# Numerator, denominator and transpose of attention among the Q projections, all operand sums on VectorE, weight sums a stage ahead

## The chip, the cores and the metric

The kernel runs on one core of one Trainium2 chip, with its own TensorE (matmuls, "PE" in the profile; its weight loads are "PEld"), VectorE ("DVE"), ScalarE ("ACT"), GpSimd ("POOL") and SyncE ("SP", which only issues transfers). The metric is the device time of one launch in microseconds. Runs shown are several executions of the same program; one further execution was recorded by the profiler, and all durations come from that one.

## What is computed

The reference is a pre-norm block with linear attention, followed by a token-mixing MLP. S = 2048 tokens, D = 1024, 32 heads of 32, F = 3584, all in bf16:

```python
qkv = (x @ wqkv) -> q, k, v per head
phi = lambda t: where(t > 0, t + 1, exp(t)) + 1e-6
pq, pk = phi(q), phi(k)
kv  = einsum("bhsd,bhse->bhde", pk, v)
z   = sum over s of pk
num = einsum("bhqd,bhde->bhqe", pq, kv)
den = einsum("bhqd,bhd->bhq", pq, z) + 1e-6
A   = (num / den) @ wo

h  = x + A(layernorm(x))
# B: layernorm again, then the MLP mixes over the tokens
u  = gelu(einsum("bsd,sf->bdf", layernorm(layernorm(h)), w1) + b1)
y  = einsum("bdf,fs->bds", u, w2) + b2
out = h + transpose(y)
```

## The kernel before

All matrices are cut into tiles of 128 partitions; S has 16 row tiles (`NS`), D has 8 (`ND`), F has 28 (14 pairs, `NFP`). One matmul instruction takes 128 x 128 weights and streams 512 columns. The stages follow each other on TensorE:

1. **K and V** (L187 to L279). Each row tile of x is loaded, normalised and transposed into `xnT`, four tiles by TensorE and twelve by a transposing DMA (L210). Then 8 matmuls for each of four column chunks give K and V. `phi_evac` (L135) makes phi with two ScalarE and two VectorE instructions. `kv_accum` sums kv and z in PSUM over all tiles.
2. **Q** (`q_unit`, L282). 32 units of 8 matmuls, (u, j) for 4 token chunks u of 512 and 8 column blocks j. Each writes `pqT[:, j, chunk u]`, which is phi(q), transposed. Four units come before the weights of attention (`ndrhs`, L304 to L306) are made. L402 to L420 issue the others: all but the last four, then two attention blocks, then the last four units.
3. **Attention and output projection** (loop at L435). For a row tile i, `attn_num_den` (L321) does 8 small matmuls into the one PSUM tile `nd_ps`, then a ScalarE copy of the denominators, a reciprocal (L339) and three multiplications (L344) on VectorE into `o_sb`. `attn_transpose` turns `o_sb` by DMA into a tile `oT`. `out_proj` (L364) seeds two PSUM tiles with x (L372), does 2 x 8 matmuls with `oT` as weights (L374), copies the result to `h_bf` (L384), takes statistics (L385, L386) and stores h to DRAM from GpSimd's queue (L390). `normalize_h` (L394) writes `hE` for even tiles and `hO` for odd ones, and after each odd tile `combine` (L126) makes the five sums that the next stage streams: on GpSimd for the first seven pairs, on VectorE for the last.
4. **W1** and 5. **W2** (`Strassen`, L464; `run_pair`, L554). Each is a product done by Strassen's scheme: per pair of output tiles seven products m1 to m7 instead of eight. Products 1, 2, 5, 6 and 7 need a sum of two weight tiles (`asum`, L474, VectorE, into the rotating tile `sa` of the pool `sapool`, or `sb2` for W2). A product is 8 matmuls in W1 and 14 in W2, so a pair is 56 or 98 matmuls, and each stage is 784. The results are added between PSUM tiles W, X, Y and Z on VectorE. In W1 the Gelu on ScalarE writes `gE` and `gO`, and `combine` on VectorE makes four of the five streamed sums of W2; the fifth, `gT1`, is made at L622 on GpSimd in 14 pieces, after W1 and before W2. The first pair of each stage is split (`first`): all k but the last of m2, m3 and m1 run ahead of the last k, which is the one that is ready last. The last product of a pair, m7, runs inside the next pair.

The order of the source is not the order of issue. At build time a planner puts the instructions of each engine in order by their readiness in its own model, with earlier lines first among those that are ready, and gives out tiles and waits. Tiles of a pool opened after another was closed reuse its memory and wait for its users: `hE`, `hO` and the W1 weights give way to the W2 weights, `gT1` and the output tiles.

The names that matter below: `pqT` (phi of q, 8 planes of 2048 columns), `o_sb`, `oT`, `hst` (statistics), `hE`/`hO`, `hT1`, `hT3`, `hT4` (combined), `sa` (weight sums), `gT1` (shown as gT_4077), `w1p`/`w2p` (weights), `hr` (h read back for the output), `xr` (x for the residual).

Of the kernel before, what the change touches and what calls it, by code (L numbers as in the profile page):

```python
# [8 lines left out]
P = 128  # L9
# [11 lines left out]
BANK = 512  # L21
# [5 lines left out]
def kernel(  # L27
# [116 lines left out]
    h_dram = [dram.tile([P, D], BF16, name=f"h_dram{i}") for i in range(NS)]  # L144
    mctx = ctx.enter_context(ExitStack())

    with ExitStack() as actx:
        a3s = actx.enter_context(tc.tile_pool(name="a3s", bufs=4))
        a3w = actx.enter_context(tc.tile_pool(name="a3w", bufs=3))
        otsb = actx.enter_context(tc.tile_pool(name="otsb", bufs=3))  # L150
# [156 lines left out]

        w1pool = mctx.enter_context(tc.tile_pool(name="w1pool", bufs=3, side="right"))
# [9 lines left out]
        with ExitStack() as a3:  # L318
# [33 lines left out]
            def attn_transpose(o_sb):  # L352
                oT = otsb.tile([P, ND, P], BF16, name="oT")
                nc.sync.dma_start_transpose(out=oT[:], in_=o_sb[:])
                return oT
# [8 lines left out]
            def out_proj(i, oT):  # L364
# [4 lines left out]
                for dc in range(NDC):  # L369
# [3 lines left out]
                    for j in range(ND):  # L373
                        nc.tensor.matmul(  # L374
                            ap_[:, 0:CW],
                            lhsT=oT[:, j, :],
                            rhs=wo_sb[:, j, dc * CW:(dc + 1) * CW],
                            start=(j == 0 and not SEED_RESIDUAL),
                            stop=(j == ND - 1 and SEED_RESIDUAL),
                            skip_group_check=SEED_RESIDUAL,  # L380
                        )
# [8 lines left out]
                nc.gpsimd.dma_start(h_dram[i][:], h_bf[:])  # L390
# [3 lines left out]
            def normalize_h(i):  # L394
                dst = hE if i % 2 == 0 else hO
                nc.vector.tensor_scalar(dst[:, i // 2, :], h_bfs.pop(i)[:], mv_all[:, i, 0:1], sc_all[:, i:i + 1], ALU.subtract, ALU.mult)  # L396
# [4 lines left out]
            HOLD = 4  # L401
            rest = q_units[4:]  # L402
            n_early = max(0, len(rest) - HOLD)
            for (u, j) in rest[:n_early]:
                q_unit(u, j)
            done_u = 0
            if len(q_units) - HOLD > 0:
                done_u = (len(q_units) - HOLD) // ND
            n_pro = min(NS, (done_u * SW) // P)
            LA3 = 2  # L410
            osb = {}
            oTs = {}
            pro_nd = min(LA3, n_pro)
            pro_tr = min(LA3 - 1, n_pro)
            for i in range(pro_nd):
                osb[i] = attn_num_den(i)
            for i in range(pro_tr):
                oTs[i] = attn_transpose(osb.pop(i))
            for (u, j) in rest[n_early:]:
                q_unit(u, j)  # L420
# [10 lines left out]
            for i in range(pro_nd, min(LA3, NS)):  # L431
                osb[i] = attn_num_den(i)
            for i in range(pro_tr, min(LA3 - 1, NS)):
                oTs[i] = attn_transpose(osb.pop(i))
# [15 lines left out]
    psy = ctx.enter_context(tc.tile_pool(name="psy", bufs=NT, space=PSUM))  # L450
    psw = ctx.enter_context(tc.tile_pool(name="psw", bufs=NT, space=PSUM))
    psz = ctx.enter_context(tc.tile_pool(name="psz", bufs=NT, space=PSUM))
    psx = ctx.enter_context(tc.tile_pool(name="psx", bufs=NT, space=PSUM))
# [5 lines left out]
    cpool = ctx.enter_context(tc.tile_pool(name="cpool", bufs=2))  # L459
    w2a = ctx.enter_context(tc.tile_pool(name="w2a", bufs=1))  # L460
    sactx = ExitStack()
    sapool = sactx.enter_context(tc.tile_pool(name="sapool", bufs=6))

    class Strassen:  # L464
        def __init__(self, wt, nk, sap, mov, evac):
            self.wt, self.nk, self.sap, self.mov, self.evac = wt, nk, sap, mov, evac
            v = wt[:].rearrange("p (k two) (h f) -> p k two h f", two=2, h=2)
            self.a11 = v[:, :, 0, 0, :]
            self.a12 = v[:, :, 1, 0, :]
            self.a21 = v[:, :, 0, 1, :]  # L470
            self.a22 = v[:, :, 1, 1, :]
            self.sa = {3: self.a11, 4: self.a22}

        def asum(self, m):  # L474
            a, b, op = {
                1: (self.a11, self.a22, ALU.add),
                2: (self.a21, self.a22, ALU.add),
                5: (self.a11, self.a12, ALU.add),
                6: (self.a21, self.a11, ALU.subtract),
                7: (self.a12, self.a22, ALU.subtract),  # L480
            }[m]
            t = self.sap.tile([P, self.nk, P], FP16, tag="sa", name="sa")
            nc.vector.tensor_tensor(t[:], a, b, op)  # L483
            self.sa[m] = t

        def mm(self, m, ps, start, stop, ks=None):
            sa, mv = self.sa[m], self.mov[m]
            for k in range(self.nk) if ks is None else ks:
                nc.tensor.matmul(  # L489
                    ps[:],  # L490
                    lhsT=sa[:, k, :],
                    rhs=mv(k),
                    start=(start and k == 0),
                    stop=(stop and k == self.nk - 1),
                    skip_group_check=True,
                )

        def m2(self, ks=None):
            if ks is None or ks[0] == 0:
                self.W = psw.tile([P, BANK], F32, tag="w", name="psW")  # L500
            self.mm(2, self.W, True, True, ks)
            if ks is None or ks[-1] == self.nk - 1:
                self.s2 = cpool.tile([P, BANK], F32, tag="s2", name="s2")
                nc.scalar.copy(self.s2[:], self.W[:])

        def m3(self, ks=None):
            if ks is None or ks[0] == 0:
                self.Z = psz.tile([P, BANK], F32, tag="z", name="psZ")
            self.mm(3, self.Z, True, True, ks)
            if ks is None or ks[-1] == self.nk - 1:  # L510
                self.d = cpool.tile([P, BANK], F32, tag="d", name="dd")
                nc.vector.tensor_tensor(self.d[:], self.Z[:], self.s2[:], ALU.subtract)

        def m1(self, ks=None):
            if ks is None or ks[0] == 0:
                self.X = psx.tile([P, BANK], F32, tag="x", name="psX")
            self.mm(1, self.X, True, True, ks)
            if ks is None or ks[-1] == self.nk - 1:
                self.Y = psy.tile([P, BANK], F32, tag="y", name="psY")
                nc.vector.tensor_tensor(self.Y[:], self.X[:], self.d[:], ALU.add)  # L520

        def m4(self):
            self.mm(4, self.W, False, True)
            self.t = cpool.tile([P, BANK], F32, tag="t", name="tt")
            nc.vector.tensor_tensor(self.t[:], self.W[:], self.d[:], ALU.add)  # L525
            self.evac(1, 0, self.W)

        def m5(self):
            self.mm(5, self.Z, False, True)
            nc.vector.tensor_tensor(self.t[:], self.t[:], self.Z[:], ALU.subtract)  # L530
            nc.vector.tensor_tensor(self.X[:], self.X[:], self.t[:], ALU.add)
            self.evac(0, 1, self.Z)

        def m6(self):
            self.mm(6, self.Y, False, True)
            self.evac(1, 1, self.Y)

        def m7(self):
            self.mm(7, self.X, False, True)
            self.evac(0, 0, self.X)  # L540

    def moving(E, O, T1, T3, T4):
        lo, hi = slice(0, CW), slice(CW, 2 * CW)
        return {
            1: lambda k: T1[:, k, :],
            2: lambda k: E[:, k, lo],
            3: lambda k: T3[:, k, :],
            4: lambda k: T4[:, k, :],
            5: lambda k: O[:, k, hi],
            6: lambda k: E[:, k, hi],  # L550
            7: lambda k: O[:, k, lo],
        }

    def run_pair(st, nxt, first, pending):  # L554
        if first:
            head = list(range(st.nk - 1))
            st.m2(head)
            st.m3(head)
            st.m1(head)
            last = [st.nk - 1]  # L560
            st.m2(last)
# [121 lines left out]
```

## Time and profile before

| What | Value |
|---|---|
| Median of 3 runs | 629.95 us (628.68 to 631.11) |
| The profiled execution | 633.12 us, of which its span (first to last instruction) is 631.3 |
| TensorE busy | 591.0 us, 94%, 2882 matmuls |
| VectorE busy | 362.6 us, 57% |
| ScalarE busy | 193.1 us, 31% |
| GpSimd busy | 71.2 us, 11% |
| Mean granted TensorE clock | 0.981 |

The page's picture of the span in 40 slices of 15.8 us shows where the engines work (tenths of each slice; PEclk is the granted clock in tenths):

```profile
PE   2998999999997988869999999999679999999997
DVE  6594112136448799876666667665935654565433
ACT  2554444446666556423223222222000000000000
POOL 1000000000000577620000000000840000000000
PEclk9999999999999899979999999999969999999999
```

A row of a view of windows reads: the stretch in us from the span's start, its length, then for PE, PEld, DVE, ACT and POOL the busy time with the number of instructions, the granted clock, and the transfers' share and rate. A row of a group reads: line, engine, operation, what is written and read, shapes, count, then busy us, mean ns of one, and the engine's idle time ahead of them with what ended it. A row of the timeline reads: start, duration, engine, line, operation, and in brackets the idle time before it. In the chain, a row is a start, a duration and what ran.

A busy TensorE is not the same as a full one: matmuls are pipelined and recorded longer than their spacing, so only the distance of starts gives the cost of one.

### The profile page before, as it was taken

Reading aid. Unit: us, or ns where it says so; the run is one execution under the profiler, and the core shown is the slowest. Engines: PE = TensorE matmul, PEld = TensorE weight load, DVE = VectorE, ACT = ScalarE, POOL = GpSimd, SP = SyncE. Lnnn points to the kernel's source line nnn. Section 1 sums busy time; section 2 is a strip of 40 time slices with the busy share of each in tenths; the row PEclk is TensorE's granted clock in tenths of the full one; section 3 lists DMA queues with packets and bytes.
Section 4 is the critical chain, followed back from the end, with each engine's and each line's share of the span. In section 5 each row is a group of like instructions: output and inputs, shape, how many; then the busy total and the mean of one; then the engine's idle time right before and its main releaser. Section 6 shows DMA issues by size and latency. Waiting matters only on the chain.

```text
span 631.3 us, 7530 instructions
## 1 busy us (share of the span) xinstructions
PE 591.0 (94%) x2882; PEld 273.0 (43%) x2882; DVE 362.6 (57%) x684; ACT 193.1 (31%) x384; POOL 71.2 (11%) x73
## 2 busy tenths in 40 slices
PE   2998999999997988869999999999679999999997
PEld 2454444444443444424444444444224444444443
DVE  6594112136448799876666667665935654565433
ACT  2554444446666556423223222222000000000000
POOL 1000000000000577620000000000840000000000
PEclk9999999999999899979999999999969999999999
DMA  9989000007009677404233234200926664351200
GB/s 292 340 198 220 1 0 1 2 0 196 6 0 213 173 165 187 114 29 122 67 105 95 66 86 114 67 2 0 239 69 175 159 166 129 98 158 44 57 26 33
DMA packets 108500, 66.56 MB, mean 105 GB/s; under 512 B 31650, under 2 KB 101296, under 8 KB 108464
## 3 DMA queue, kind: packets, MB, share of 16 engines
q1 hardware_dynamic: 107120, 61.88, 38.2%
q0 software_dynamic: 1344, 4.21, 1.8%
q8 instruction: 22, 0.36, 0.3%
q14 instruction: 14, 0.11, 0.1%
HBM read 50.34 MB, written 8.39 MB: 93 GB/s over the span
## 4 chain that ended last, share of the span: by engine, by line
PE 75%; DVE 10%; POOL 3%; DMA 3%; ACT 2%; issue 1%; POOLq 0%; DVEq 0%; SPq 0%
PE psW L489 15%; PE psX L489 15%; PE psZ L489 15%; PE acc_t L215 12%; PE acc_t L285 8%; PE psY L489 8%; POOL gT_4077 L622 3%; DVE hE L396 3%; DVE hst L385 3%; DVE o_sb L344 2%; DMA oT<-o_sb 1%; PE acc_t L374 1%; DMA x_sb<-in_A_x_dram 1%; DVE st L195 1%; DMA xnT<-xn 1%
## 5 line engine op out<-in xcount | busy, mean ns | idle before, releaser
L489 PEld LDWEIGHTS <-sa 128*128 128x128 f16 x1120 | 110.0, 98 | 152.1 <-issue 20.8
L215 PE MATMUL acc_t<-wkv,xnT 128*128 128x512 bf16 x512 | 115.2, 383 | 0.0
L215 PEld LDWEIGHTS <-xnT 128*128 128x128 bf16 x512 | 49.9, 99 | 56.8 <-issue 1.1
L140 DVE TENSOR_SCALAR e_sb<-e_sb 128x512 bf16<-128x512 bf16 x64 | 18.7, 292 | 84.4 <-ACT e_sb L137 84.3
L374 PE MATMUL acc_t<-wo_sb,oT 128*128 128x512 bf16 x256 | 59.4, 387 | 3.4 <-DMA oT<-o_sb 3.4
L483 DVE TENSOR_TENSOR sa<-w1p 128x1024 f16<-128x1024 bf16 x70 | 47.7, 684 | 21.2 <-PE psX L489 12.4
L285 PE MATMUL acc_t<-xnT,wq_sb 128*128 128x512 bf16 x256 | 56.1, 379 | 0.0
L483 DVE TENSOR_TENSOR sa<-w2p 128x1792 f16<-128x1792 bf16 x40 | 47.8, 1202 | 14.4 <-PE psW L489 13.7
L137 ACT ACTIVATE e_sb<-acc_t 128x512 bf16<-128x512 f32 x64 | 38.2, 597 | 52.5 <-PE acc_t L215 31.8
L622 POOL TENSOR_TENSOR gT_4077<-gE,gO 128x512 f16<-128x512 f16 x14 | 21.2, 1548 | 170.9 <-PE psX L489 170.9
L374 PEld LDWEIGHTS <-oT 128*128 128x128 bf16 x256 | 24.8, 99 | 31.9 <-DMA oT<-o_sb 4.1
L139 ACT ACTIVATE r_sb<-acc_t 128x512 bf16<-128x512 f32 x64 | 37.9, 592 | 0.0
L285 PEld LDWEIGHTS <-wq_sb 128*128 128x128 bf16 x256 | 24.9, 98 | 29.3
L489 PE MATMUL psX<-gT_4077,sa 128*128 128x512 f16 x112 | 28.8, 394 | 9.3 <-POOL gT_4077 L622 8.0
L489 PEld LDWEIGHTS <-w2p 128*128 128x128 bf16 x224 | 22.3, 100 | 27.7 <-issue 2.2
L525 DVE TENSOR_TENSOR tt<-psW,dd 128x512 f32<-128x512 f32 x22 | 15.2, 692 | 31.9 <-PE psW L489 31.8
L489 PEld LDWEIGHTS <-w1p 128*128 128x128 bf16 x224 | 21.9, 98 | 26.4
L489 PE MATMUL psW<-hE,sa 128*128 128x512 f16 x112 | 28.3, 395 | 4.4 <-DVE hst L385 4.4
L520 DVE TENSOR_TENSOR psY<-psX,dd 128x512 f32<-128x512 f32 x22 | 15.4, 699 | 25.2 <-PE psX L489 25.2
L489 PE MATMUL psZ<-hT_1947,w1p 128*128 128x512 f16 x112 | 26.8, 379 | 0.9 <-POOL hT_1947 L130 0.9
L489 PE MATMUL psX<-hT_1946,sa 128*128 128x512 f16 x112 | 27.0, 383 | 0.0
L489 PE MATMUL psW<-gT_2812,w2p 128*128 128x512 f16 x112 | 26.6, 391 | 0.0
(205 smaller groups left out, 712.4 us busy)
## 6 DMA issues: line engine op xcount, KB each, us to landing
w1p<-in_B_w_dram SPq DMA_DIRECT2D x14, 1024.0 KB, 5.7
w2p<-in_B_w_dram SPq DMA_DIRECT2D x8, 1792.0 KB, 8.4
x_sb<-in_A_x_dram SPq DMA_DIRECT2D x16, 256.0 KB, 6.3
xr<-in_A_x_dram SPq DMA_DIRECT2D x16, 256.0 KB, 2.9
wkv<-in_A_wqkv_dram SPq DMA_DIRECT2D x3, 1024.0 KB, 12.0
wq_sb<-in_A_wqkv_dram SPq DMA_DIRECT2D x2, 1024.0 KB, 12.0
wo_sb<-in_A_wo_dram SPq DMA_DIRECT2D x2, 1024.0 KB, 8.7
wkv<-in_A_wqkv_dram SPq DMA_DIRECT2D x2, 512.0 KB, 6.3
```

The lines of the kernel that those rows point to most:

```text
L137: nc.scalar.activation(e_sb[:], src, ACT.Exp)
L139: nc.scalar.activation(r_sb[:], src, ACT.Relu)
L140: nc.vector.tensor_scalar(e_sb[:], e_sb[:], 1.0, PHI_EPS, ALU.min, ALU.add)
L215: nc.tensor.matmul(pp[:, 0:CW], lhsT=xnT[:, kt, i * P:(i + 1) * P], rhs=wkv[:, kt, c * CW:(c + 1) * CW], start=(kt == 0), stop=(kt == ND - 1),
L285: nc.tensor.matmul(qp[:, 0:SW], lhsT=wq_sb[:, kt, j * P:(j + 1) * P], rhs=xnT[:, kt, u * SW:(u + 1) * SW], start=(kt == 0), stop=(kt == ND ...
L374: nc.tensor.matmul(ap_[:, 0:CW], lhsT=oT[:, j, :], rhs=wo_sb[:, j, dc * CW:(dc + 1) * CW], start=(j == 0 and not SEED_RESIDUAL), stop=(j = ...
L385: nc.vector.bn_stats(st[:, dc, :], ap_[:, 0:CW])
L396: nc.vector.tensor_scalar(dst[:, i // 2, :], h_bfs.pop(i)[:], mv_all[:, i, 0:1], sc_all[:, i:i + 1], ALU.subtract, ALU.mult)
L483: nc.vector.tensor_tensor(t[:], a, b, op)
L489: nc.tensor.matmul(ps[:], lhsT=sa[:, k, :], rhs=mv(k), start=(start and k == 0), stop=(stop and k == self.nk - 1), skip_group_check=True,)
L520: nc.vector.tensor_tensor(self.Y[:], self.X[:], self.d[:], ALU.add)
L622: nc.gpsimd.tensor_tensor(gT1[:, p, :], gE[:, p, 0:CW], gO[:, p, CW:2 * CW], ALU.add)
```

## The change

The change touches four things.

- **Attention.** The Q units run in one loop. After every second unit of the chunks u = 1, 2 and 3 comes `attn(i)` (numerator, denominator, division and transpose) for one row tile of the chunk before: 12 of the 16. The last four stand in the projection loop at i = 0, 2, 4 and 6. The transposing DMA writes into `pqT`, over the columns it came from; the tile `oT` and its pool are gone, and `out_proj` takes its weights from `pqT`.
- **Sums.** `combine` is on VectorE for all pairs. `gT1` is made on VectorE in two pieces of seven tiles, instead of 14 on GpSimd. h is stored from SP's queue.
- **Weight sums ahead.** One pool `sapool` with 5 slots (before: 6, and 6 more for W2) is opened before the W1 weights and lives through both MLP stages. The sums of the first W1 pair stand in the projection loop at i = 10; those of the first W2 pair stand around the last m7 of W1.
- **Waits on memory.** Some pools wait by tile (`reuse_waits="tile"`), PSUM pools are opened in another order, `cpool` has one copy of each tile instead of two, the first W2 pair is not split, and `hr` is loaded at the start of its pair. The class `Strassen` moves up in the file; but for `asum` and the pool argument it is unchanged.

```diff
+            def attn_transpose(i, o_sb):
+                nc.sync.dma_start_transpose(out=pqT[:, :, i * P:(i + 1) * P], in_=o_sb[:])
...
-                            lhsT=oT[:, j, :],
+                            lhsT=pqT[:, j, i * P:(i + 1) * P],
...
-                nc.gpsimd.dma_start(h_dram[i][:], h_bf[:])
+                nc.sync.dma_start(h_dram[i][:], h_bf[:])
...
-                    combine(nc.vector if q == NSP - 1 else nc.gpsimd, hE[:, q, :], hO[:, q, :], hT1[:, q, :], hT3[:, q, :], hT4[:, q, :])
+                    combine(nc.vector, hE[:, q, :], hO[:, q, :], hT1[:, q, :], hT3[:, q, :], hT4[:, q, :])
+
+            def attn(i):
+                attn_transpose(i, attn_num_den(i))
+
+            TPC = SW // P
+            for (u, j) in q_units[4:]:
                 q_unit(u, j)
+                if u >= 1 and j % 2 == 1:
+                    attn((u - 1) * TPC + j // 2)
             xctx.close()
...
             for i in range(NS):
-                if i + LA3 < NS:
-                    osb[i + LA3] = attn_num_den(i + LA3)
-                if i + LA3 - 1 < NS:
-                    oTs[i + LA3 - 1] = attn_transpose(osb.pop(i + LA3 - 1))
+                if i % 2 == 0 and i // 2 < TPC:
+                    attn(NS - TPC + i // 2)
                 if i + 2 < NS:
                     load_xr(i + 2)
-                out_proj(i, oTs.pop(i))
+                out_proj(i)
                 if i >= 2:
                     normalize_h(i - 2)
+                if i == NS - 6:
+                    cur = mk1(0)
+                    for m in (2, 1, 5, 6, 7):
+                        cur.asum(m)
...
+    psy = ctx.enter_context(tc.tile_pool(name="psy", bufs=NT, space=PSUM, reuse_waits="tile"))
+    psx = ctx.enter_context(tc.tile_pool(name="psx", bufs=NT, space=PSUM, reuse_waits="tile"))
+    psw = ctx.enter_context(tc.tile_pool(name="psw", bufs=NT, space=PSUM, reuse_waits="tile"))
+    psz = ctx.enter_context(tc.tile_pool(name="psz", bufs=NT, space=PSUM, reuse_waits="tile"))
...
-    cpool = ctx.enter_context(tc.tile_pool(name="cpool", bufs=2))
+    cpool = ctx.enter_context(tc.tile_pool(name="cpool", bufs=1))
...
+    nxt = mk2(0)
+    for m in (2, 1, 5, 6):
+        nxt.asum(m)
     pend.m7()
-    sactx.close()
+    nxt.asum(7)
     mctx.close()
...
-    for p in range(NFP):
-        nc.gpsimd.tensor_tensor(gT1[:, p, :], gE[:, p, 0:CW], gO[:, p, CW:2 * CW], ALU.add)
+    half = NFP // 2
+    for sl in (slice(0, half), slice(half, NFP)):
+        nc.vector.tensor_tensor(gT1[:, sl, :], gE[:, sl, 0:CW], gO[:, sl, CW:2 * CW], ALU.add)
...
-        run_pair(cur, nxt, p == 0, pend)
+        cur.evac.prefetch()
+        run_pair(cur, nxt, False, pend)
```

More of the change, by code (lines that the diff above doesn't have):

```diff
@@ L362, in load_xr, with out_proj @@
                 xrs[i] = xr
-            def out_proj(i, oT):
+            def out_proj(i):
                 xr = xrs.pop(i)
@@ L458 @@
     gT4 = gpool.tile([P, NFP, CW], FP16, name="gT4")
-    cpool = ctx.enter_context(tc.tile_pool(name="cpool", bufs=2))
+    cpool = ctx.enter_context(tc.tile_pool(name="cpool", bufs=1))
     w2a = ctx.enter_context(tc.tile_pool(name="w2a", bufs=1))
[L461 to L540, printed above, removed]
@@ L597 @@
-    cur = mk1(0)
-    for m in (2, 1, 5, 6, 7):
-        cur.asum(m)
+    hmov.update(moving(hE, hO, hT1, hT3, hT4))
     pend = None
```

243 lines of the change are left out of this document (140 added, 103 removed).

## The prediction

> **What bounds the kernel now.** I first cut the run at its stage borders (windows: length, then busy time and instructions of PE, PEld, DVE, ACT and POOL, then the granted clock).
>
> ```profile
> span 631.3 us, 7530 instructions
> 136.48:193.97 57.49, 57.38 (x290) 26.79 (x289) 30.07 (x98) 35.96 (x68) 0.00 (x0) 1.00 0.27 64
> 193.97:266.89 72.92, 64.25 (x363) 30.88 (x361) 63.19 (x122) 41.33 (x104) 42.02 (x45) 0.98 0.74 175
> 266.89:274.07 7.18, 1.84 (x9) 0.69 (x8) 6.51 (x6) 1.46 (x4) 6.13 (x7) 0.78 0.16 63
> 274.07:443.70 169.63, 169.63 (x778) 76.56 (x778) 108.69 (x194) 47.67 (x72) 0.00 (x0) 0.99 0.26 69
> 443.70:465.93 22.23, 12.90 (x44) 4.19 (x42) 15.57 (x10) 1.27 (x2) 21.17 (x14) 0.76 0.77 201
> 465.93:627.60 161.67, 161.66 (x743) 72.75 (x740) 82.32 (x105) 4.11 (x7) 0.00 (x0) 0.99 0.38 104
> ```
>
> Q projections, most of W1 and most of W2 have a full TensorE. Time is lost in three places: the output projection (193.97 to 266.89), the start of W1 and the start of W2. These are also the only places where GpSimd works and where the clock falls below 0.98. To price the losses I need the real cost of a matmul, since busy time overlaps. From the chain and the timeline:
>
> ```profile
> 286.59 1.73 PE psX L489 x8
> 440.26 1.73 PE psY L489 x8
> 242.95 3.62 PE L374 MATMUL acc_t<-wo_sb,oT 128*128 128x512 bf16 x16
> 246.41 0.63 PE L323 MATMUL nd_ps<-ndrhs,pqT 128*128 128x132 bf16 x8
> 246.88 3.61 PE L374 MATMUL acc_t<-wo_sb,oT 128*128 128x512 bf16 x16
> 443.56 1.46 PE L489 MATMUL psZ<-gT_2811,w2p 128*128 128x512 f16 x6
> ```
>
> Between the first two rows lie 89 blocks of eight: 153.67/712 = 0.216 us per 512-column matmul. One numerator and denominator set takes 0.47 us (246.41 to 246.88). So:
> - output projection: 256 matmuls (55.3) and 13 of the 16 sets (6.1) make 61.4 of 72.92: **11.5 lost**;
> - W1, from 266.89 to 443.56: 784 matmuls are 169.3 of 176.7: **7.4 lost**;
> - W2, from 443.56 to 627.60: 169.3 of 184.0: **14.7 lost**.
>
> Together 33.6 us. Who holds TensorE there (waits in the two stretches, then VectorE's groups from 193.97 to 274.07):
>
> ```profile
> PEld L323 <- DVE o_sb L344: 8.7, 8, 2.1
> PE acc_t L374 <- DMA oT<-o_sb: 3.4, 1, 3.4
> PE psX L489 <- POOL gT_4077 L622: 8.0, 8, 1.6
> L385 DVE BATCH_NORM_STATS2 hst<-acc_t 128x6 f32<-128x512 f32 x32 | 22.0, 690 | 6.4 <-ACT h_bf L384 6.4
> L396 DVE TENSOR_SCALAR hE<-h_bf,mv_all,sc_all 128x1024 f16<-128x1024 bf16 x8 | 19.2, 2394 | 0.6 <-ACT sc_all L389 0.6
> L396 DVE TENSOR_SCALAR hO<-h_bf,mv_all,sc_all 128x1024 f16<-128x1024 bf16 x7 | 3.7, 529 | 0.0
> L386 DVE BATCH_NORM_AGGREGATE mv_all<-hst 128x2 f32<-128x12 f32 x16 | 2.7, 166 | 0.1
> ```
>
> VectorE bounds the output projection: 63.19 of 72.92 us busy. The same normalisation takes 529 ns for hO and 2394 for hE, which is written while GpSimd combines the previous pair. At the W2 start TensorE waits for GpSimd's 14 sums of gT1.
>
> **The change, part by part.** *Attention among the Q projections.* Twelve of the 16 sets move in front of the projection, nine more than now. TensorE pays 9 x 0.47 = 4.2 us there and saves it later: nothing net. One set stands behind every two Q units, so every 16 x 0.216 + 0.47 = 3.9 us. VectorE adds per set:
>
> ```profile
> 248.46 0.36 DVE L339 RECIPROCAL rd<-dn 128x36 f32<-128x36 f32 x1
> 248.91 1.35 DVE L344 TENSOR_TENSOR o_sb<-nd_ps,rd 128x384 bf16<-128x384 f32 x3
> xnT<-xn SPq DMA_TRANSPOSE x12, 3.6
> ```
>
> That is 1.71; nine more are 15.4, and 30.07 + 15.4 = 45.5 of the stage's new 61.7. VectorE's idle half is the cover; a set that overran its 3.9 us would cost the excess twelve times. The set uses one PSUM tile, so it returns after 0.47 + 0.36 + 1.35 and ScalarE's part: below 3.9, cost 0 (bounds 0 to 4). The transposes now write back into pqT; the nearest row is xnT, with the same strided destination, 3.6 us to landing. They land far ahead of their use, so the 3.4 us wait on oT goes.
>
> *Output projection, after.* VectorE keeps statistics 22.0, aggregation 2.7, 16 normalisations at 0.53 (8.5) and four attention blocks (4 x 1.71 = 6.8). It takes over the 40 combines that GpSimd had (35 of them) or VectorE itself (five):
>
> ```profile
> 275.44 0.43 DVE L129 TENSOR_TENSOR hT_1946<-hE,hO 128x512 f16<-128x512 f16 x1
> 276.78 0.42 DVE L133 TENSOR_TENSOR hO<-hO 128x512 f16<-128x512 f16 x1
> L483 DVE TENSOR_TENSOR sa<-w1p x70: 627/684/693, 193.7 to 430.0; 128x1024 f16<-128x1024 bf16 x70
> ```
>
> 40 x 0.42 = 16.8. Sum 56.8 us, or 60.2 if the five first weight sums (5 x 0.68) fall here too; I take them to be issued in the Q stage, as six already run ahead of their place in the code. TensorE needs 55.3 + 4 x 0.47 = 57.2. Consecutive VectorE rows start before the last one's recorded end (five combines from 275.44 to 277.20 are 1.76 us, not 2.1), and today's iteration from 242.95 to 246.88 ran at TensorE's own 3.93 us (16 x 0.216 + 0.47). So TensorE bounds, narrowly. Left over I take 2 us (bounds 0, and 6 where VectorE's durations count in full: the first rival).
>
> *Stores of h on SP instead of GpSimd's queue.* Sixteen issues at 0.33 us, the price of a load there, are 5.3 us of SP in a stage of 57.
>
> ```profile
> 249.19 0.33 SPq L361 DMA_DIRECT2D xr<-in_A_x_dram  x1
> xr<-in_A_x_dram SPq DMA_DIRECT2D x16, 256.0 KB, 2.9
> 193.70 1.29 DVE L483 TENSOR_TENSOR sa<-w1p 128x1024 f16<-128x1024 bf16 x2 [0.19 <-PE acc_t L285]
> ```
>
> Each waits for its copy on ScalarE; behind it stand the next loads of x, used two iterations (7 us) later and landing in 2.9. Cost 0, at worst one late load, 2.9. (The third row is L483 running ahead of its place in the code: engines follow a planned order by readiness.)
>
> *Start of W1.* What delays it today is one hE:
>
> ```profile
> 268.14 4.67 DVE L396 TENSOR_SCALAR hE<-h_bf,mv_all,sc_all 128x1024 f16<-128x1024 bf16 x1 [0.60 <-ACT sc_all L389]
> 272.73 1.28 DVE L385 BATCH_NORM_STATS2 hst<-acc_t 128x6 f32<-128x512 f32 x2
> 271.38 1.14 POOL L133 TENSOR_TENSOR hO<-hO 128x512 f16<-128x512 f16 x1
> ```
>
> It ends as GpSimd's last combine does, and goes with it. After the last projection matmul the chain is then: ScalarE's copy (0.8, my estimate from ScalarE's 0.69 row below and a 0.1 handover), and as today from the second statistics (about 273.35) to the last combine's end at 277.20, 3.85: 4.6 us. Over it lie the first seven k of m2, m3 and m1, 21 matmuls or 4.5 us. Left over 1 us (bounds 0 to 4.6, where the heads were spent earlier as fill).
>
> *Start of W2.* The sums 2, 1, 5 and 6 of the first W2 pair come before the last m7, in a pair that has no successor's sums to make. gT1 moves to VectorE as two sums over 3584 elements:
>
> ```profile
> L483 DVE TENSOR_TENSOR sa<-w2p x40: 1079/1082/2036, 443.8 to 604.1; 128x1792 f16<-128x1792 bf16 x40
> 443.95 21.17 POOL L622 TENSOR_TENSOR gT_4077<-gE,gO 128x512 f16<-128x512 f16 x14 [170.92 <-PE psX L489]
> L520 DVE TENSOR_TENSOR psY<-psX,dd 128x512 f32<-128x512 f32 x22 | 15.4, 699 | 25.2 <-PE psX L489 25.2
> 443.76 0.69 ACT L589 ACTIVATE gE<-psX,b_sb 128x512 f16<-128x512 f32 x1 [1.04 <-PE psX L489]
> 443.79 4.37 SPq L120 DMA_DIRECT2D w2p<-in_B_w_dram  x2
> 454.49 0.43 SPq L629 DMA_DIRECT2D hr_4099<-h_dram_94  x1
> hr_4099<-h_dram_94 SPq DMA_DIRECT2D x1, 256.0 KB, 5.0
> ```
>
> By the slope from 1024 (684 ns) to 1792 elements (1082) one is 1.08 + 1792 x 0.52 ns = 2.0 us, two 4.0. VectorE after m7: Gelu 0.9, combine 4 x 0.42, sum 7 1.08, gT1 4.0: 7.7 us. TensorE first has m2, m3 and m4, 42 matmuls or 9.07 us. Nothing is left over; I take 0.5 (bounds 0 to 5).
>
> *The rest.* One sum slot fewer: in W1, sum 7 of the next pair waits for this pair's m7, which ends 16 matmuls (3.45 us) into the next pair. Behind it on VectorE stands the difference after m3, due after 24 (5.2): 0. Single copies of s2, d and t are read and rewritten on VectorE in order, but for s2, which ScalarE rewrites a pair later: 0. A W2 pair keeps five sums of 1.08 and nine passes over PSUM of about 0.7, 11.7 us of VectorE, under 98 x 0.216 = 21.2 of TensorE. The PSUM pools in another order, waiting by tile: m2 and m3 of the first W1 pair no longer wait for the last statistics; that gain is inside the sums above.
>
> **Sum.** 33.6 - 2 - 1 - 0.5 = 30.1 us saved. The profiled execution took 633.12 (span 631.3 and 1.8 around it), so 603.0. The runs' median, 629.95, lies 3.2 below; from it 599.9, and I say **600**.
>
> **Weighed against the Trainium skill.** hE's row above has 2394 ns on average, where hO has 529, so contention costs 19.2 - 8 x 0.53 = 15.0 us now. The page "SBUF — State Buffer", section "Who interferes with whom", says that VectorE in a two-port mode and GpSimd hold the shared ports one instruction at a time, and that the second fully blocks until the first finishes. By that, a block is at most one GpSimd combine, so at most 8 x 1.14 = 9 us would be returned, against the row's 15. The row decides: 4.67 us are four combines. If only 9 of the 15 were contention, each hE would still take 1.27 us, VectorE would hold 62.8 us of the new projection, 5.6 over TensorE, and the time would be 606; by the rows it is 600.
>
> **Rivals.** *VectorE becomes the bound of the projection.* For: 60.2 against 57.2 if the sums land there, and pairs of iterations are uneven (a combine adds 2.1 us to every second). Against: durations overlap. If they did not, the stage lasts 60.2 plus 2.5 before the first statistics (8 matmuls and the copy), 5.5 more than TensorE's; with the start chain exposed (4.6 - 1) the time is 600 + 5.5 - 2 + 3.6 = **607**. The page "TensorE: Matmul & The Clock Gate", section "Architectural detail: the array is 16× 32×32, not 1× 128×128", says VectorE is strictly first in, first out; no row contradicts it, and it is what would turn one late operand into this case.
>
> *A late load at the W2 start.* The first store of the output sum waits for hr on VectorE. Today the second hr landed at 454.49 + 5.0, 15.7 us after the W2 loads' issue at 443.79; If that holds from m7's end, the store starts at 15.7; m6, after 70 matmuls (15.1), needs Y, and between lie the store and L520, about 0.7 each. So the load is late by 15.7 - (15.1 - 1.4) = 2 us: **602**, inside the forecast's range. Against: waiting by tile, the W2 loads may start before m7 ends.
>
> *The move does not happen.* The planned order leaves the sets where they are. Then VectorE still holds 22.0 + 2.7 + 8.5 + 16.8 + 13 x 1.71 = 72.2 us there, as now, and only the two starts gain (7.4 - 1 and 14.7 - 0.5): **609**. For: 13 sets stand in the projection today though three Q chunks were long done. Against: the code issued them late then; their inputs are ready early.
>
> *Slower: the transposes in pqT count as writing the whole tile.* Their destination has rows in all eight planes. If a Q unit's write of other columns had to wait for them, each set would be a serial chain, 0.47 + 0.36 + 1.35 + 3.6 = 5.8 against 3.9 us. Twelve times 1.9 is 23; the four in the projection hold its matmuls for 5.3 each, 21: **644**. It decides once these waits pass 30 us. Against it, xnT does the same while other columns are read:
>
> ```profile
> 30.00:58.00 28.00, 26.14 (x151) 13.00 (x149) 22.79 (x56) 15.03 (x42) 0.00 (x0) 1.00 0.95 205
> ```
>
> TensorE is 93% busy there (26.14 of 28), with the transposes of later tiles landing meanwhile.
>
> **Chances.** Forecast (596 to 604, with the late load) 0.68; VectorE bound 0.20; move not done 0.07; slower 0.05. The low end is all 33.6 us and the runs' spread: 595. The high end is the VectorE case with the unknowns at their upper bounds, 607 + 4: 612. A measurement of this kernel tells about 0.5% from no change. Faster by more 0.94, within 0.02, slower 0.04 (rounded from the cases, with a little of the third taken as no change).
>
> **What would show it.** Right: no POOL sums; hE at 0.53 us; 12 sets before the Q projections end; projection 57 to 60 us; W1 and W2 each 169 to 171 us; no wait on gT1. Wrong: VectorE at over 95% in the projection with TensorE waiting for hst; TensorE waiting for a transpose among the Q units; m1 of the first W2 pair waiting; a clock below 0.95 in the W2 start. The prediction falls if the Q stage grows by more than 4.2 us beyond its 57.5.

## The result, and the profile after

The changed kernel takes 600.62 us (median of 4 runs, 599.77 to 602.42), beside 630.53 us (628.68 to 631.83) for the kernel before: ratio 0.9532, 95% interval 0.9497 to 0.9566. It was predicted at 600, between 595 and 612.

The page of its profiled execution (601.21 us), first two parts:

```profile
span 599.4 us, 7482 instructions
PE 579.7 (97%) x2882; PEld 271.4 (45%) x2882; DVE 355.9 (59%) x721; ACT 192.8 (32%) x384; POOL 1.8 (0%) x8
...
PE   2999999999899999999999999999999999999997
...
POOL 1000000000000000000000000000000000000000
PEclk9999999999999999999999999999999999999999
```

The two dips of the TensorE row in the picture before are gone, and so is GpSimd after the first slice. In the same stretches as before (windows: length, then busy time and instructions of PE, PEld, DVE, ACT and POOL, the clock, the transfers):

```profile
0.00:134.00 134.00, 121.87 (x665) 60.23 (x666) 55.53 (x152) 61.32 (x128) 1.83 (x8) 1.00 0.45 124
134.00:197.85 63.85, 61.91 (x363) 31.06 (x362) 46.16 (x138) 37.69 (x77) 0.00 (x0) 1.00 0.46 92
197.85:257.11 59.26, 57.33 (x291) 26.81 (x289) 48.34 (x117) 40.21 (x98) 0.00 (x0) 1.00 0.65 182
257.11:424.60 167.49, 167.49 (x777) 75.93 (x776) 112.80 (x199) 47.55 (x72) 0.00 (x0) 1.00 0.29 78
424.60:446.80 22.20, 22.20 (x104) 10.06 (x103) 16.49 (x21) 1.96 (x3) 0.00 (x0) 1.00 0.94 246
446.80:595.70 148.90, 148.90 (x690) 67.34 (x688) 75.78 (x96) 4.11 (x7) 0.00 (x0) 1.00 0.35 98
```

From the first W1 matmul (257.11) to the last of W2 (595.70) TensorE is busy without a gap: 338.6 us for 2 x 784 matmuls, 0.216 each. Before it was 360.7 (266.89 to 627.60).

Not all that before lost was waiting. In three stretches of the kernel before, behind TensorE's waits on oT, on hst and on gT1, the granted clock (the number before the transfers' share) is 0.50 or 0.51:

```profile
206.10:209.50 3.40, 3.40 (x10) 1.20 (x9) 2.62 (x6) 1.73 (x5) 0.00 (x0) 0.51 0.90 215
274.40:277.20 2.80, 2.80 (x8) 1.06 (x7) 2.31 (x6) 0.39 (x2) 0.00 (x0) 0.50 0.00 0
464.40:468.70 4.30, 4.30 (x11) 1.47 (x10) 3.30 (x4) 0.59 (x1) 0.73 (x1) 0.50 0.00 0
```

There 25 matmuls start 0.43 us apart instead of 0.216, which makes 5.3 of the 33.6 us that the prediction counted as lost. The changed kernel has 1.00 in every stretch above. That it was the waits that lowered the clock was not tested.

The balance of the two profiled spans, 631.3 and 599.4:

| Stretch | Before | After | Difference |
|---|---|---|---|
| up to the Q projections | 136.5 | 134.0 | -2.5 |
| Q projections | 57.5 | 63.9 | +6.4 |
| output projection | 72.9 | 59.3 | -13.7 |
| W1 and W2 | 360.7 | 338.6 | -22.1 |

The first line is not the change: every kernel profiled later, those built from the kernel before among them, begins its Q projections between 132.4 and 134.2 us. The profiled execution of before, 2.6 us above its median, had lost that at its start. The change itself gives 29.4.

The waits of TensorE in the changed kernel (what was waited for: us in total, times, longest), those from the Q loop on:

```profile
...
PE acc_t L527 <- ACT acc_t L525: 1.9, 1, 1.9
PE nd_ps L478 <- DVE pqT L141: 1.4, 1, 1.4
...
PE nd_ps L478 <- DVE o_sb L499: 0.5, 1, 0.5
```

The waits of before on the transposed attention (oT), on hst and on sums at the starts of W1 and W2, gT1 among them, have no row any more; two new ones have come. The first stands in the projection, in the timeline from 200 us:

```profile
200.92 4.37 SPq L508 DMA_TRANSPOSE pqT<-o_sb  x1
...
205.39 0.53 SPq L543 DMA_DIRECT2D h_dram_93<-h_bf  x1
...
206.01 1.28 SPq L508 DMA_TRANSPOSE pqT<-o_sb  x1
...
207.34 0.57 SPq L514 DMA_DIRECT2D xr<-in_A_x_dram  x1
...
210.65 1.11 ACT L525 CAST acc_t<-xr 128x512 f32<-128x512 bf16 x2 [2.27 <-DMA xr<-in_A_x_dram]
...
211.29 3.61 PE L527 MATMUL acc_t<-wo_sb,pqT 128*128 128x512 bf16 x16 [1.93 <-ACT acc_t L525]
```

In SP's queue a transpose whose issue takes 4.37 us (2.6 us behind a W2 load of 1.8 MB), the first store of h and a second transpose stand ahead of the load of x. ScalarE waits for that load until 210.65 and seeds PSUM late, and TensorE loses 1.93 us. The other is in the Q loop:

```profile
145.85 5.02 SPq L112 DMA_DIRECT2D w1p<-in_B_w_dram  x1
...
151.11 0.69 DVE L192 TENSOR_TENSOR sa<-w1p 128x1024 f16<-128x1024 bf16 x1 [3.20 <-DMA w1p<-in_B_w_dram]
...
153.93 0.23 PE L478 MATMUL nd_ps<-ndrhs,pqT 128*128 128x132 bf16 x1 [1.40 <-DVE pqT L141]
...
158.15 0.65 PE L478 MATMUL nd_ps<-ndrhs,pqT 128*128 128x132 bf16 x8 [0.54 <-DVE o_sb L499]
```

VectorE stands 3.2 us behind a W1 weight sum whose weights have not landed. The phi of a Q unit, and with it an attention set, comes late. The Trainium skill, page "TensorE: Matmul & The Clock Gate", section "Architectural detail: the array is 16× 32×32, not 1× 128×128", says that VectorE takes its instructions strictly in order; these rows agree.

At the W2 start (timeline):

```profile
419.61 16.34 SPq L120 DMA_DIRECT2D w2p<-in_B_w_dram  x3
...
424.60 1.03 PE L198 MATMUL psW<-gE,sa 128*128 128x512 f16 x4
...
429.35 3.19 PE L198 MATMUL psZ<-gT_2804,w2p 128*128 128x512 f16 x14
429.41 3.95 DVE L626 TENSOR_TENSOR gT_4069<-gE,gO 128x3584 f16<-128x3584 f16 x2
...
435.39 3.19 PE L198 MATMUL psX<-gT_4069,sa 128*128 128x512 f16 x14
```

The two sums of gT1 take 3.95 us and end at 433.4, 2 us before m1 reads them at 435.39. Further W2 loads are issued at 419.61 and W2's first matmuls run at 424.60, both ahead of W1's last product.

### The profile page after: what moved, and what is told of

Read it like the earlier page. It is cut to its first block, busy times and chain, and to the rows that moved or that the text cites. A ratio compares the mean times of both kernels' runs of the same rounds, so it can differ in the third digit from the quotient of the medians.

```text
span 599.4 us, 7482 instructions
## 1 busy us (share of the span) xinstructions
PE 579.7 (97%) x2882; PEld 271.4 (45%) x2882; DVE 355.9 (59%) x721; ACT 192.8 (32%) x384; POOL 1.8 (0%) x8
## 4 chain that ended last, share of the span: by engine, by line
PE 64%; DVE 1%; DMA 1%; ACT 0%; SPq 0%; issue 0%; DVEq 0%
PE psX L198 16%; PE psZ L198 16%; PE psW L198 16%; PE psY L198 8%; PE acc_t L527 8%; DMA xr<-in_A_x_dram 1%; DVE o_sb L499 0%; DVE hst L538 0%; SPq L508 0%; ACT acc_t L525 0%; PE nd_ps L478 0%; DVE ot_5013 L163 0%; DVE rd L494 0%; ACT hln_l L541 0%; ACT dn L486 0%
## 5 line engine op out<-in xcount | busy, mean ns | idle before, releaser
L140 DVE TENSOR_SCALAR e_sb<-e_sb 128x512 bf16<-128x512 bf16 x64 | 18.6, 290 | 72.9 <-ACT e_sb L137 72.9
L527 PE MATMUL acc_t<-wo_sb,pqT 128*128 128x512 bf16 x256 | 56.2, 379 | 1.9 <-ACT acc_t L525 1.9
L439 PE MATMUL acc_t<-xnT,wq_sb 128*128 128x512 bf16 x256 | 57.5, 379 | 0.0
L192 DVE TENSOR_TENSOR sa<-w2p 128x1792 f16<-128x1792 bf16 x40 | 43.4, 1084 | 10.1 <-PE psW L198 7.6
L527 PEld LDWEIGHTS <-pqT 128*128 128x128 bf16 x256 | 24.8, 98 | 31.1 <-issue 2.2
L538 DVE BATCH_NORM_STATS2 hst<-acc_t 128x6 f32<-128x512 f32 x32 | 22.1, 695 | 8.9 <-ACT h_bf L537 8.9
L198 PE MATMUL psW<-hE,sa 128*128 128x512 f16 x112 | 26.6, 379 | 0.0
L198 PE MATMUL psX<-hT_2116,sa 128*128 128x512 f16 x112 | 26.6, 379 | 0.0
L198 PE MATMUL psW<-hT_2118,w1p 128*128 128x512 f16 x112 | 26.5, 379 | 0.0
L198 PE MATMUL psZ<-hO,sa 128*128 128x512 f16 x112 | 26.5, 379 | 0.0
```

The source lines that it names most:

```text
L140: nc.vector.tensor_scalar(e_sb[:], e_sb[:], 1.0, PHI_EPS, ALU.min, ALU.add)
L192: nc.vector.tensor_tensor(t, a, b, op)
L198: nc.tensor.matmul(ps[:], lhsT=sa[:, k, :], rhs=mv(k), start=(start and k == 0), stop=(stop and k == self.nk - 1), skip_group_check=True,)
L439: nc.tensor.matmul(qp[:, 0:SW], lhsT=wq_sb[:, kt, j * P:(j + 1) * P], rhs=xnT[:, kt, u * SW:(u + 1) * SW], start=(kt == 0), stop=(kt == ND ...
L527: nc.tensor.matmul(ap_[:, 0:CW], lhsT=pqT[:, j, i * P:(i + 1) * P], rhs=wo_sb[:, j, dc * CW:(dc + 1) * CW], start=(j == 0 and not SEED_RES ...
L538: nc.vector.bn_stats(st[:, dc, :], ap_[:, 0:CW])
```

## The experiments

Twelve kernels were run, each built from before or after with a part of the change done or undone, or with one edit more. Stage lengths go from first matmul to first matmul; the last column ends at W2's last matmul. In one kernel, the one with the attention late, W1 starts before the projection ends, and its second border lies inside the projection. The times of before, of the changed kernel, of the stores on GpSimd and of the two kernels with six xr buffers are medians of four or five executions; the others are of one, and one execution carries about 2 us of spread. The stages within one trace are sharper.

| Kernel | Time, us | Q | projection | W1 and W2 |
|---|---|---|---|---|
| before | 630.53 | 57.5 | 72.9 | 360.7 |
| before + gT1 on VectorE | 622.41 | 57.6 | 72.4 | 352.8 |
| before + combines on VectorE | 625.31 | 57.6 | 74.9 | 353.1 |
| before + attention among Q | 633.72 | 61.6 | 72.1 | 360.8 |
| before + attention among Q + stores on SP | 619.39 | 61.6 | 62.1 | 357.8 |
| after | 600.62 | 63.9 | 59.3 | 338.6 |
| after, attention late | 603.86 | 57.6 | 64.7 | 342.5 |
| after, combines on GpSimd | 601.48 | 61.9 | 60.3 | 340.9 |
| after, stores on GpSimd | 599.49 | 62.3 | 57.4 | 339.2 |
| after, combines and stores on GpSimd | 616.34 | 62.5 | 69.8 | 345.5 |
| after, gT1 on GpSimd | 604.62 | 63.3 | 58.8 | 343.9 |
| after, W2 sums behind gT1 | 599.89 | 63.3 | 59.1 | 338.6 |
| after + six xr buffers | 597.82 | 63.2 | 57.2 | 338.6 |
| after + six xr buffers + W1 sums later | 597.32 | 62.1 | 57.1 | 338.6 |

**One part alone, and one part undone.** gT1 alone, in the kernel before:

```diff
-    for p in range(NFP):
-        nc.gpsimd.tensor_tensor(gT1[:, p, :], gE[:, p, 0:CW], gO[:, p, CW:2 * CW], ALU.add)
+    half = NFP // 2
+    for sl in (slice(0, half), slice(half, NFP)):
+        nc.vector.tensor_tensor(gT1[:, sl, :], gE[:, sl, 0:CW], gO[:, sl, CW:2 * CW], ALU.add)
```

> The kernel before with one part of the change: gT1 made on VectorE in two pieces. Theory A (GpSimd's 14 sums are what the W2 start waits for): VectorE after m7 has the Gelu's 0.9 us, combine 1.7, gT1 4.0 and the weight sums 2 and 1 at 1.08 each, 8.8 us, of which the head of m3 covers 2.8; from the last m7's end to the end of W2 176 to 178 us instead of 184.0, time 622 to 625. Theory B (the wait is on memory that is given back late, and GpSimd only fills it): 182 or more, time 628 to 631.

622.41: as theory A had it. W2 lasts 175.6 us, from 441.3 to its last matmul at 616.9, and still loses 6.3 to the 169.3 of a full TensorE. The timeline shows to what:

```profile
441.53 4.39 SPq L120 DMA_DIRECT2D w2p<-in_B_w_dram  x2
...
446.45 6.09 DVE L483 TENSOR_TENSOR sa<-w2p 128x1792 f16<-128x1792 bf16 x6
447.68 5.71 PE L489 MATMUL psW<-gE,sa 128*128 128x512 f16 x13 [3.20 <-DVE sa L483]
```

The weight sums come behind gT1, and TensorE waits 3.20 us for the first one. The 13 matmuls behind that wait then take 5.5 us, at a granted clock of 0.50 (447.68 to 453.20), 2.7 more than at 0.216 each. Further W2 loads are issued only when W1's last product has run (441.53; in the changed kernel 5 us ahead of the stage border), but no wait on a W2 load shows here. Combines alone:

```diff
-                    combine(nc.vector if q == NSP - 1 else nc.gpsimd, hE[:, q, :], hO[:, q, :], hT1[:, q, :], hT3[:, q, :], hT4[:, q, :])
+                    combine(nc.vector, hE[:, q, :], hO[:, q, :], hT1[:, q, :], hT3[:, q, :], hT4[:, q, :])
```

> The kernel before with combine on VectorE for all pairs. Theory A (VectorE's amount of work bounds the projection): hE falls to 0.53 us, but 35 combines come, 76.0 - 15.0 + 14.7 us of VectorE; the projection stays at 70 to 75 us and only the W1 start gains, 4 to 6 us: 624 to 627. Theory B (contention with GpSimd bounds the projection): it falls to 62 to 65 us, time 613 to 617.

625.31, also A: hE falls to about 0.52 us and the loss at the W1 start is gone (W1 169.2), but the projection is 2 us longer, not shorter. There TensorE waits for late transposes (first row); with the attention put back late in the changed kernel it waits less for them (second row, of that kernel):

```profile
PE acc_t L374 <- DMA oT<-o_sb: 9.1, 9, 3.5
```

```profile
PE acc_t L527 <- DMA pqT<-o_sb: 4.7, 5, 2.7
```

That second kernel takes the loop of before for the attention:

```diff
-                if u >= 1 and j % 2 == 1:
-                    attn((u - 1) * TPC + j // 2)
+                if n == len(q_units) - 8:
+                    osb[0] = attn_num_den(0)
+                    osb[1] = attn_num_den(1)
+                    attn_transpose(0, osb.pop(0))
...
-                if i % 2 == 0 and i // 2 < TPC:
-                    attn(NS - TPC + i // 2)
+                if i + 2 < NS:
+                    osb[i + 2] = attn_num_den(i + 2)
+                if i + 1 < NS:
+                    attn_transpose(i + 1, osb.pop(i + 1))
```

> The changed kernel with attention back in the projection loop (14 of 16 sets there), transposes still in place, all sums on VectorE. Theory A (VectorE's amount bounds): 22.0 + 2.7 + 8.5 + 16.8 + 14 x 1.71 = 74 us of VectorE in the projection, which lasts 70 to 75 us instead of 59.3, Q 57 to 58: time 605 to 611. Theory B (once GpSimd is silent, TensorE bounds either way): projection 62 to 64, time 599 to 602.

603.86, between the theories: the move of the attention, which names the change, is worth some 3 us once the other parts are there. The stage lengths hide how: 16 projection matmuls run behind the border, so the projection takes 68.6 us to its end, 9.3 more than in the changed kernel, whose Q loop is 6.3 longer. Why this projection is still shorter than that of the combines alone was not taken apart; the kernels also differ in the tile of the transposes and in the queue of the stores. The attention moved alone, in before:

> The kernel before with attention among the Q units and the transposes in place, combine still on GpSimd. Theory A: VectorE in the projection falls by 9 x 1.71 = 15.4 us to 60.6, Q grows by 4.2 to 6 us, projection 60 to 64, both later starts as before: 620 to 624. Theory B (contention bounds it, moved work or not): projection 66 to 70, Q longer, 627 to 631. If the in-place transposes made Q units wait: Q over 75 us.

```diff
+            for (u, j) in q_units[4:]:
+                q_unit(u, j)
+                if u >= 1 and j % 2 == 1:
+                    attn((u - 1) * TPC + j // 2)
...
-                if i + LA3 < NS:
-                    osb[i + LA3] = attn_num_den(i + LA3)
-                if i + LA3 - 1 < NS:
-                    oTs[i + LA3 - 1] = attn_transpose(osb.pop(i + LA3 - 1))
+                if i % 2 == 0 and i // 2 < TPC:
+                    attn(NS - TPC + i // 2)
```

633.72, on B's side and beyond it: the Q loop grows by 4 us and the projection stays at 72. So I took it that hE beside GpSimd's combines holds the projection by itself, and put the combines back on GpSimd in the changed kernel (the edit above, backwards):

> The changed kernel (601) with the combines of h back on GpSimd, all else kept, so attention stays among the Q projections. Theory A (two bounds, either of which alone holds the output projection near 72 us: hE waiting for GpSimd, or attention on VectorE): hE at 2.4 us again, the projection 59.3 to 70-73 us, the start of W1 loses 4 to 7.5 us: 616 to 622. Theory B (the parts add up, as the run with the combines alone gained 4.5 us): 605 to 607, projection 59 to 62.

**A miss for both theories: 601.48.** In the time, the combines on GpSimd cost 0.9 us, which one execution can't tell from nothing. By the stages they cost 3.3 (projection 1.0, W1 and W2 2.3), and a Q loop 2.0 shorter hides most of it; theory A wanted 15 or more. hE has 1140 ns on average there, between the 524 of the changed kernel and the 2770 of the kernel with the attention moved alone. Something else in before makes hE so slow. Its timeline had shown it:

```profile
213.77 1.15 POOL L130 TENSOR_TENSOR hT_1947<-hE,hO 128x512 f16<-128x512 f16 x1
214.84 1.47 DVE L396 TENSOR_SCALAR hE<-h_bf,mv_all,sc_all 128x1024 f16<-128x1024 bf16 x1
214.88 1.15 POOL L131 TENSOR_TENSOR hT_1948<-hO,hE 128x512 f16<-128x512 f16 x1
215.99 1.33 POOL L132 TENSOR_TENSOR hE<-hE 128x512 f16<-128x512 f16 x1
...
220.90 1.14 POOL L130 TENSOR_TENSOR hT_1947<-hE,hO 128x512 f16<-128x512 f16 x1
221.99 0.56 POOL L390 DMA_DIRECT2D h_dram_97<-h_bf  x1
222.58 1.17 POOL L131 TENSOR_TENSOR hT_1948<-hO,hE 128x512 f16<-128x512 f16 x1
223.36 2.89 DVE L396 TENSOR_SCALAR hE<-h_bf,mv_all,sc_all 128x1024 f16<-128x1024 bf16 x1
223.69 1.16 POOL L132 TENSOR_TENSOR hE<-hE 128x512 f16<-128x512 f16 x1
224.79 1.16 POOL L133 TENSOR_TENSOR hO<-hO 128x512 f16<-128x512 f16 x1
```

In the first pair no store stands among the five sums of the combine: hE takes 1.47 us and gets in after one of them. In the second a store of h (221.99) stands between the second and the third sum: hE takes 2.89 us and ends after the last. Three runs tried that reading. Both parts put back on GpSimd in the changed kernel, beside the stores alone:

```diff
-                nc.sync.dma_start(h_dram[i][:], h_bf[:])
+                nc.gpsimd.dma_start(h_dram[i][:], h_bf[:])
```

> The changed kernel with the combines of h and the stores of h both on GpSimd, as before; each of the two alone gave 601.5 and 599.5 against 600.6. Theory A (a store issued between two combines in GpSimd's queue is what lets hE wait for all that follow: 2.9 to 3.2 us each, against 1.1 on average without the store): hE at 2.4 us or more on average, the projection 66 to 73 us, 608 to 616. Theory B (the order of the changed kernel hides hE, store or not): hE at 1.1 to 1.5, 600 to 603.

> The changed kernel with the stores of h issued from GpSimd's queue as before. Theory A (the stores on SP stand in front of the loads of x, and the 1.9 us wait of the projection is theirs): 598 to 600 against 600.6, the wait on xr at 211 us gone. Theory B (SP is held by the transposes and the W2 load, the stores ask nothing): no difference within 1 us, the wait stays.

And the stores alone put on SP, in the kernel with the attention moved (the same edit, backwards):

> The kernel before with the attention among the Q projections, which alone took 633.7, and the stores of h on SP; the combines stay on GpSimd. Theory A (the store in GpSimd's queue held the projection at 72 us): hE at 1.1 to 1.5 us on average, the projection 59 to 62, the start of W1 losing 2 to 4 instead of 7.6: 615 to 620. Theory B (the combines on GpSimd hold it, wherever the store is issued): hE above 2, 628 to 633.

All three came out on A's side, the time of 616.34 and the 62.1 us of the last kernel's projection just past its ranges. Each part alone on GpSimd: 601.48 and 599.49 (ratio to before 0.9512, 0.9492 to 0.9533); both together: 616.34. From the other side, the stores on SP take the kernel with the moved attention from 633.72 to 619.39. The group of hE on VectorE (count, then busy us and mean ns) in the kernel with both on GpSimd, in the one with the attention moved alone, and in that with the stores taken off:

```profile
L549 DVE TENSOR_SCALAR hE<-h_bf,mv_all,sc_all 128x1024 f16<-128x1024 bf16 x8 | 23.4, 2919 | 1.0 <-ACT sc_all L542 1.0
```

```profile
L394 DVE TENSOR_SCALAR hE<-h_bf,mv_all,sc_all 128x1024 f16<-128x1024 bf16 x8 | 22.2, 2770 | 0.6 <-ACT sc_all L387 0.6
```

```profile
L394 DVE TENSOR_SCALAR hE<-h_bf,mv_all,sc_all 128x1024 f16<-128x1024 bf16 x8 | 9.8, 1221 | 0.6 <-ACT sc_all L387 0.6
```

The rows of each hE sharpen the reading: what sets the slow ones apart is how shortly before them a store was issued, more than its place among the sums. In before, in the kernel with the attention moved alone and in the one with both on GpSimd, the 17 hE of 2.88 us or more start 0.26 to 1.75 us after a store of h; the four others that run beside GpSimd's sums start 2.97 us or more after one and take 0.76 to 1.47. In the row of 4.67 us that the prediction shows, the store stood ahead of the pair's first sum (266.40), not among the sums.

With both on GpSimd, TensorE waits in the projection for PSUM tiles that ScalarE seeds late behind VectorE's statistics:

```profile
PE acc_t L527 <- ACT acc_t L525: 9.8, 13, 1.8
```

The run with the stores alone on GpSimd also answers for the wait on xr: that wait of TensorE is gone there (ScalarE still waits 2.2 us for a block of x, until 206.6, but TensorE does not), so the store in SP's queue had its part in it.

**The W2 start.** gT1 back on GpSimd in the changed kernel, and the sums of the first W2 pair moved behind gT1:

> The changed kernel (601) with the sums of gT1 on GpSimd as before, all else kept; the weight sums of the first W2 pair stay ahead of the last m7. Theory A (gT1 alone made the W2 start late): TensorE waits for gT1 at psX again, 8 to 15 us lost: 609 to 616. Theory B (the sums made ahead give m2, m3 and m4 and the fill enough cover): 601 to 604.

604.62, between the two: W1 and W2 lose 5.3 us, not the 14.7 that the W2 start lost before. TensorE's waits on gT1 at the W2 start of this kernel come to no more than

```profile
PE psX L198 <- POOL gT L625: 2.5, 4, 0.7
```

since GpSimd, waiting by tile, begins its 14 sums at 419.54, ahead of the stage, where before it began at 443.95, behind it.

```diff
-    for m in (2, 1, 5, 6):
-        nxt.asum(m)
     pend.m7()
-    nxt.asum(7)
...
+    for m in (2, 1, 5, 6, 7):
+        nxt.asum(m)
     cur = nxt
```

> The changed kernel with the five weight sums of the first W2 pair made behind the sums of gT1 instead of ahead of the last m7; gT1 stays on VectorE. Theory A (the early sums carried part of the W2 start, as the run with gT1 alone shows, where TensorE waited for a sum): 4 to 8 us lost, 604.5 to 608.5, TensorE waiting for sa behind gT1. Theory B (gT1 was the whole loss): 600 to 602.

599.89, as B had it, but this does not decide: the trace has four of the five sums ahead of gT1 all the same (414.82, 420.61, 422.33, 423.94; gT1 from 425.27), as the planner puts work in by readiness. What the early sums are worth alone stays open.

**The two waits that were left.** More buffers for x, so that a further block is loaded ahead of the W2 load:

```diff
-                xr = a3w.tile([P, D], BF16, name="xr")
+                xr = xrp.tile([P, D], BF16, name="xr")
```

> The changed kernel with six buffers for the loaded blocks of x in a pool of their own, so that a load can be issued before the block two ahead has been used. Theory A (the wait of 1.9 us on xr in the projection comes from loads that are issued too late for want of a buffer): 598.5 to 599.2, no wait on xr. Theory B (the load is late because SP is held up, whatever the buffers): within 0.7 us of the changed kernel.

597.82 (597.16 to 598.39), ratio 0.9481 (0.9464 to 0.9499), somewhat below what A gave; no wait on xr is left. Then the W1 sums as well, held behind the phi of Q unit (1, 6), which is not the last unit, as the text on record has it, but late enough for their load:

```diff
+                if (u, j) == (1, 6):
+                    after_ins = phi_ins.ins
...
+                    with tc.issue_after(after_ins):
+                        for m in (2, 1, 5, 6, 7):
+                            cur.asum(m)
```

> The changed kernel with six buffers for the blocks of x (597.8 alone) and the first five weight sums of W1 issued behind the last Q unit. Theory A (the 1.9 us that TensorE waits for a set among the Q units come from VectorE standing behind a sum whose load has not landed): no PE wait on pqT or o_sb in the Q stage, 596 to 597, below both kernels. Theory B (the sums fill VectorE in the projection or the wait moves): 597.5 to 600.

The wait on pqT is gone and 0.3 us on o_sb is left, and the Q loop is 62.1 us long, but the time, 597.32 (595.91 to 598.16, ratio 0.9490, 0.9474 to 0.9507), can't be told from that with the buffers alone. Both run below the two kernels of the case by their medians; the gain over the changed kernel, about 3 us, is at the edge of what is measured.

## Why the prediction was right, point by point

- **The sum.** 30.1 us were forecast, and 29.9 came between the medians. Left over after the change are 1.9 us of waits in the projection and 1.9 in the Q loop, 3.8; the prediction left 2 + 1 + 0.5. That the totals agree so closely is partly luck: the Q stage cost 2.2 us more than booked, and the starts of W1 and W2 lost nothing where 1.5 had been left.
- **Q stage.** That a set returns within 3.9 us, at cost 0, held but for two of them. The step that failed is "five first weight sums ... I take them to be issued in the Q stage", booked at nothing: they were issued there, but the first stood 3.2 us for its load at VectorE's head. The stage grew by 6.4 us where 4.2 was the mark at which the prediction was to fall; the 1.9 us of waits make up most of the rest.
- **Projection.** 59.3 us, within 57 to 60, with four sets and TensorE as the bound, as argued. The 2 us left over were to come from VectorE; they came from the late xr, the "late load, 2.9" that the stores on SP were given as the worst case. The worst case happened, at 1.9. The size of the 2 us was right, the cause was not.
- **Starts of W1 and W2.** Nothing was lost where 1.5 had been left. gT1 took 3.95 us against 4.0. The granted clock, 0.78 and 0.76 in the prediction's rows of the two starts, is 1.00 there, which keeps clear of its sign of being wrong (below 0.95).
- **Contention.** That hE would return to 0.53 was right, and so was the 4.67 us row over several combines. The reason given, the combines on GpSimd, is only half: it takes a store issued shortly before in the same queue as well, and the change removed both. Without the store hE waits for about one combine. The Trainium skill, page "SBUF — State Buffer", section "Who interferes with whom", says that whoever issues first keeps the shared pair for the whole instruction and the other fully blocks; hE rows of up to 1.47 us, with no store shortly before, agree with that. With the store, 2.88 to 5.08 us do not, and the measurement decides.
- **Rivals.** VectorE did not become the bound: 48.3 of 59.3 us busy. Its trigger, one late operand at the head of its queue, did come, and cost 1.9 us instead of 7. The late hr load did not show. "The move does not happen" was priced at 609; the run with the attention late gives 603.9. The added-up durations overstate the stage: they gave 72.2 us, and VectorE is busy 60.7 there, of 69.0. In the changed kernel TensorE has no wait on a transpose: the rival with tile-wide waits had no ground.
- **What the prediction did not see** is that its losses were not separate. Done alone in before, the parts gave 7.4 (gT1), 4.5 (combines) and minus 3.9 us (attention) against the 629.83 of before on the same chip, 8 in all; the whole change gave 30. In the kernel before, each of two things held the projection at 72 to 75 us without the other: hE behind GpSimd's combines and stores (72.1 with the attention moved away), and the attention's late sets and transposes (74.9 with hE at 0.52). The second needs other parts of before as well, since late attention in the changed kernel takes 68.6 us. At the W2 start, gT1 on GpSimd and weight sums made only there overlapped: gT1 alone gave 8.4 of 14.7, and without it the rest gave 9.4 (14.7 - 5.3). How much of that rest is the early sums, and how much GpSimd's earlier start, is not shown.

## What to carry to other kernels

Where two causes hold the same stage, undoing one alone shows nothing, and where a loss needs two things together, as hE needed combines and stores, putting one back shows nothing either. Test a part from both ends, alone in the old kernel and taken out of the new one, before calling it worthless or decisive. A mean over a group hides its cases: of hE's times in the kernel before, those of 0.95 and 1.47 us told more than the average of 2.39. When work is moved onto an in-order queue, look at what its first instruction waits for: a sum standing for its load, or a store ahead of a load, cost more here than the work moved.

## What the hardware did that I had not expected

- A transfer issued by GpSimd between its tensor operations changes how VectorE gets in: 0.95 to 1.47 us for a 128x1024 scaling beside GpSimd's combines where the last store was issued 2.97 us or more before, 2.88 to 5.08 where it was issued at most 1.75 us before, in before and in the kernel with both put back. These stores also go by another DMA queue (q0, software_dynamic: 1344 packets, and 64 once they are on SP). That the store decides is shown from both sides; what in the chip does it isn't.
- Issuing a transposing transfer takes SP 1.23 us (median), but 2.77 to 4.37 for one issued 2.6 to 3.4 us behind a 1.8 MB load, in 13 of 14 kernels. In the other, with the attention late, it came 5.5 us behind the load and took 1.28.
- GpSimd also slows VectorE's weight sums: 1.44 to 2.03 us beside the 14 sums of gT1, against 1.08.
